# Seven more pairs of warming products in the prologue of an mLSTM and feed-forward kernel

## The chip, the cores and the metric

The kernel runs on one core of a Trainium2 chip. The metric is the device time of one execution, in microseconds (us). Before the change the median of three runs is 470.69 us.

## The reference

Four batches of eight heads run an mLSTM over 768 tokens with a head size of 40. Its gated output, 3072 tokens of 320 channels, goes through a feed-forward block with 2048 hidden channels and a leaky activation.

```python
for t in range(S):
    m_new = np.maximum(f_gate[:, :, t] + m, i_gate[:, :, t])
    f_stab = np.exp(f_gate[:, :, t] + m - m_new)
    i_stab = np.exp(i_gate[:, :, t] - m_new)
    m = m_new
    C = f_stab[:, :, None, None] * C + i_stab[:, :, None, None] * np.einsum('bhd,bhe->bhde', vt, kt)
    n = f_stab[:, :, None] * n + i_stab[:, :, None] * kt
    h_tilde = np.einsum('bhde,bhe->bhd', C, qt)
    nq = np.einsum('bhd,bhd->bh', n, qt)[:, :, None]
    denom = np.maximum(np.abs(nq), 1.0)
    y[:, :, t] = (1.0 / (1.0 + np.exp(-o_gate[:, :, t]))) * h_tilde / denom
# y becomes x: (B*S, H*D)
h = x @ w_in
out = (np.maximum(h, 0.0) + alpha * np.minimum(h, 0.0)) @ w_out
```

## The kernel before

The tokens are cut into chunks of 128, six to a batch. For a chunk the recurrence is written as products: scores (keys by queries) weighted by decays, times the values, plus what the state at the chunk's start gives. Two chunks form a group of 256 tokens, and each group then goes through the feed-forward block, whose products are each split into high and low parts (`WH`, `WL`, `OH`, `OL`, `XH`, `XL`, `gh`, `gl`).

Every engine works through its instructions in a fixed order. The string `ORDER` names the steps of the first six chunks and the first two groups in the order in which they are issued, a repeated `PATTERN` goes on from there, and `pin` chains all instructions in that order. A step may issue instructions on several engines; each engine runs its own in the order of the string, and waits on the others through semaphores.

The change lies in the prologue, the first 20 us or so, before any feed-forward product. Steps there, with their names in `ORDER`, the lines in the profile and the tiles:

- `warm2` issues two bf16 products of the identity with itself, 128 x 256, into a PSUM tile `warm` (L152) that nobody reads. `warm18` issues 18 at the very start.
- `qT0`, `kT0`, `qT1`, `kT1`: transposes of a chunk's queries or keys on TensorE (L245, tile `pqk`). `qc1`, `kc1`: their copies on ScalarE (L987, L301, L302; tiles `qf`, `kf`).
- `sp01`, `sp00`, `sp11`, `sp10`: the spreads of the decays. The digits are the chunk and the parity of the heads. Each is one bf16 "bar" product over 512 columns with full rows (L92) that blanks the future, and four float32 products that spread a row of `g_L` over the partitions, with 32 rows (L1001; the trace has two records for each); both go into a tile `pb`.
- `ex01` and the like: the exponentials of a spread on ScalarE (L1030, tile `E`).
- `bTt`, `wTt`, `eTt`: small transposes of the gates (L959, tiles `ps_gb`, `ps_gw`, `ps_ge`), and `bTc`, `wTc`, `eTc`: their copies on VectorE (L963, tile `gates`).
- `L1` (VectorE, L1111), `wd0` (the weighted keys `kd`, L160), `i00j` (unpacking a piece of `w_in`, VectorE L816), `gmd` (`g_gd`, VectorE L1139) and `gmm` (its product `pg` on TensorE, L1146).
- `sc00`, `sc01`, `sc11`, `sc10`: the scores (L1055, tile `pS`, with 104 rows). `um0`: the first state update (L182, tile `pu`), `uc0` its copy (VectorE, L196, tile `C`).

Tiles `pqk`, `pb`, `ps_g*`, `pu`, `pg` share four PSUM buffers in turn. The tile `warm` has a buffer of its own.

The warming products come from these lines:

```python
    def dense(dst, k):
        x = ident.bitcast(BF16)
        for _ in range(k):
            nc.tensor.matmul(dst[:, : 2 * P], x[:, :P], x, start=True, stop=True)
```

Of the kernel before, what the change touches and what calls it, by code (L numbers as in the profile page):

```python
# [17 lines left out]
def kernel(ctx: ExitStack, tc: tile.TileContext, q, k, v, i_gate, f_gate, o_gate, w_in, w_out, alpha, out):  # L18
# [575 lines left out]
    def first_stacks():  # L594
# [25 lines left out]
    OBA = range(0)  # L620
    FILL = {}
    ORDER = """warm18 dq0 Cz warm2 warm2 warm2 qT0 warm2 sca0 lf0a kT0 i00d lf0z lf0b li0 L0 sca1 bj0 dq1 warm2 qc0 kc0 sp01 eeL i00s
        lf1a wt0 qT1 qc1 bTt bTc ex01 sp00 sp11 r0d lf1b ewj wTt wTc ex00 sp10 ex11 kT1 i00y L1 li1 do0 dv0 kfz i01d
        eTt ex10 wd0 dq2 gma i00j sc00 o0d lpa sc01 um0 kc1 gmd gmm sc11 eTc eel bj1 og1 r0s uc0 fm1 wtl wg01 sc10 ewl
        lpb i11d wd1 alT wg00 gmc qT2 i01s glt ft1 wg10 glc alC dL lpc lpd lpe qc2 warm2 wg11 dv1 um1 uc1 i00h i01x
        i01j kT2 kc2 i00p o0s o0x sp20 v0 r0y r0j gr0 sp21 fm2 dq3 ex20 warm2 o0j r0h i01h ft2 i01p ex21 o0h warm2 gg0
        r0l gx0 i11s sc20 wg20 v1 ta1 gr1 qT3 qc3 i11x gp0 x0 xa0 sc21 dL4 gg1 gx1 gp1 kT3 wg21 x1 xa1 o1d wd3 xd0 r0H
        xd1 wd2 sq30 ey30 r0L i11j ex40 o0l F0 U00 i20d i10d R00 S00 kc3 v2 ta2 um2 uc2 o1s o1y U01 dq4 i10s i10x i10j
        sq31 gr2 o1j i11k i11l ey31 qT4 G00 ex41 fm3 ft3 sc30 K00 wg30 i10h um3 uc3 D00 R01 kT4 i20s do1 S01 qc4 wd4
        kc4 o1h i20x sc31 wg31 dv2 um4 uc4 i20j og2 o2d i20h gg2 i10p fm4 o1l o5d sc41 wg41 G01 K01 i21d gx2 r2d sc40  # L630
        i20p o2s o2x dq5 wg40 o5s o5x v3 ta3 o2j gr3 gg3 o2h o5j r2s dL5 o4d r2x o2l U02 o3d r2j gx3 gp3 R02 gp2 i21s
        v4 ft4 ta4 qT5 qc5 r2H ex50 r2h r2p U03 x2 R03 S02 G02 x3 dq6 i21y i21j r2L i31d fm5 ft5 xa2 xd2 i21h i21p dv3
        i30d kT5 kc5 K02 S03 o4s o4y D01 G03 wd6 K03 o3s o3y o3j D02 do2 dL7 ex51 o7d o4j o6d U04 R04 S04 o3h xa3 V05
        r05 o3p o4h sc50 o4p sc51 G04 i31s i31x xd3 s05 wg51 um6 uc6 K04 gr4 wg50 F1 U10 U11 R10 S10 og3 gg4 gx4 dL6
        gp4 R11 S11 G10 o5h o5p v5 K10 D10 U12 ta5 G11 g05 K11 vp0 i31j i30s i30x gr5 gg5 U13 i31h i30j R12 i30h D11
        S12 i31l G12 gx5 gp5 K12 D12 R13 dq7 S13 o7s i30l U06 o7x do3 o7j N05 G13 K13 D13 tp0 o6s tp1 o6x R06 tp2 x4
        x5 o6j o6h vp1 U07 o7h tp3 D03 D04 D05 R07 S06 G06 S07 o6l xa5 xd5 xa4 xd4 G07 K06 K07 D06 o7l D07 Z0"""
    PATTERN = """og.-1 ua.0 m1.0 V4<< tf.1 ub.0 vb.1 xn.-1 V5<< tg.1 g2<< m0.0 N2<< vc.1 c1.0 r4<< vb.0 d1.0 xp.-1 th.1 h1.0 ti.1 uc.0
        s4<< ud.0 D2<< ue.0 U6<< g4<< l1.0 g3<< N3<< uf.0 r5<< lG.-1 c0.0 vd.1 X:-1 vc.0 ua.1 lG.2 sh.1 ub.1 s5<< N4<<
        oa.0 R6<< d0.0 g5<< ug.0 h0.0 l0.0 uc.1 V7<< N5<< xa:-1 vd.0 D3<< D4<< D5<< S6<< ta.2 tb.2 xb:-1 uh.0 lL.2  # L640
# [687 lines left out]
```

## Time and profile before

| what | value |
| --- | --- |
| median of 3 runs | 470.69 us (470.62 to 471.09) |
| profiled execution: time | 472.36 us |
| profiled execution: span | 470.7 us |
| mean granted TensorE clock over the span | 0.989 |
| TensorE busy (products; weight loads) | 464.5 us; 452.1 us |
| VectorE, ScalarE, GpSimd busy | 310.1, 314.4, 308.7 us |
| bytes moved by DMA | 61.61 MB |

The span runs from the first to the last instruction of the profiled execution; its time includes what lies around the span. Engines in the profile's rows: PE is TensorE, DVE VectorE, ACT ScalarE, POOL GpSimd, SP SyncE, which issues the transfers here. A row such as `pb<-g_L,ident` names the tile written and the tiles read. "Idle before" in brackets is how long the engine had stood still and who released it. The granted clock is the share of TensorE's full clock that the throttle let through. Products are pipelined, so that the ends that the timeline models overlap a little; in the chain of waits they are cut to what each adds.

### The profile page before, as it was taken

The page shows a single profiled execution, that of the slowest core. Times are in us where ns is not written, and L with a number is a line of the kernel's source. Part 1 is how long each engine was busy: PE and PEld are TensorE (multiplying, and loading weights), DVE is VectorE, ACT ScalarE, POOL GpSimd, SP SyncE. Part 2 cuts the span into 40 slices and gives each one's busy share as a digit, 9 for nine tenths or more (in the row PEclk, how much of TensorE's full clock was granted, in tenths as well). Part 3 has the DMA queues.
Part 4 walks back from the last instruction along what each step waited for, and adds up shares of the span by engine and source line. Part 5 has one row for each costly group of instructions (what it writes and reads, how often), then busy time and mean ns, then how long its engine had stood idle before and what let it go on. Part 6 is the DMA issues. An engine that isn't in the chain of part 4 may idle for free.

```text
span 470.7 us, 11787 instructions
## 1 busy us (share of the span) xinstructions
PE 464.5 (99%) x4420; PEld 452.1 (96%) x4420; DVE 310.1 (66%) x659; ACT 314.4 (67%) x714; POOL 308.7 (66%) x398
## 2 busy tenths in 40 slices
PE   8999999999999999999999999999999999999997
PEld 6899999999999999999999999999999999999996
DVE  4589899767875775775675675676576676663321
ACT  4778998868858658559659659558658658423332
POOL 7634657664789589479689589479689586324231
PEclk9599999999999999999999999999999999999999
DMA  9996997659683574688583584579672352000000
GB/s 171 244 246 126 225 272 227 122 121 222 124 176 98 122 163 112 116 185 171 122 164 109 125 149 124 116 158 187 134 155 90 95 110 64 1 29 1 29 2 28
DMA packets 156163, 61.61 MB, mean 131 GB/s; under 512 B 140154, under 2 KB 145834, under 8 KB 156106
## 3 DMA queue, kind: packets, MB, share of 16 engines
q1 hardware_dynamic: 156026, 60.75, 58.6%
q8 instruction: 35, 0.57, 0.5%
q14 instruction: 22, 0.18, 0.1%
q10 hardware_dynamic: 80, 0.11, 0.1%
HBM read 36.90 MB, written 4.03 MB: 87 GB/s over the span
## 4 chain that ended last, share of the span: by engine, by line
PE 92%; DVE 3%; ACT 2%; DMA 1%; issue 1%; SPq 1%; DVEq 0%; ACTq 0%
PE po L733 35%; PE ph L696 6%; PE ph L701 5%; PE ph L702 5%; PE ph L699 5%; PE ph L697 5%; PE ph L698 5%; PE ph L700 5%; PE ph L703 5%; PE pH L360 4%; PE pS L461 3%; PE pS L1055 2%; PE pu L182 2%; PE pH L321 1%; PE p L550 1%; PE pI L385 1%
## 5 line engine op out<-in xcount | busy, mean ns | idle before, releaser
L722 POOL TENSOR_TENSOR gl<-g,gh 128x512 fp32r<-128x512 f32 x74 | 95.7, 1295 | 37.9 <-ACT gh L720 30.9
L733 PE MATMUL po<-OH,gh 128*128 128x320 f32 x368 | 110.7, 312 | 0.0
L733 PE MATMUL po<-OL,gh 128*128 128x320 f32 x368 | 109.3, 309 | 0.0
L706 ACT ACTIVATE g<-ph 128x512 f32<-128x512 f32 x96 | 57.3, 597 | 76.1 <-PE ph L703 71.9
L711 DVE SCALAR_TENSOR_TENSOR g<-g,oma,ph 128x256 f32<-128x256 f32 x148 | 63.6, 471 | 36.0 <-ACT g L706 36.0
L733 PEld LDWEIGHTS po<-OH,gh 128*128 128x128 f32 x368 | 69.1, 188 | 0.0
L733 PE MATMUL po<-OH,gl 128*128 128x320 f32 x368 | 69.1, 309 | 0.0
L733 PEld LDWEIGHTS po<-OL,gh 128*128 128x128 f32 x368 | 69.1, 188 | 0.0
L696 PE MATMUL ph<-XH,WH 128*128 128x256 f32 x192 | 58.0, 302 | 0.4 <-DVE g L711 0.4
L733 PEld LDWEIGHTS po<-OH,gl 128*128 128x128 f32 x368 | 57.9, 188 | 0.3 <-DVE gl L722 0.3
L701 PE MATMUL ph<-XL,WH 128*128 128x256 f32 x192 | 54.3, 283 | 0.0
L702 PE MATMUL ph<-XL,WH 128*128 128x256 f32 x192 | 54.2, 282 | 0.0
L699 PE MATMUL ph<-XH,WL 128*128 128x256 f32 x192 | 54.2, 282 | 0.0
L697 PE MATMUL ph<-XH,WH 128*128 128x256 f32 x192 | 54.1, 282 | 0.0
L698 PE MATMUL ph<-XH,WL 128*128 128x256 f32 x192 | 54.1, 282 | 0.0
L703 PE MATMUL ph<-X2L,W 128*128 128x256 f32 x192 | 53.4, 278 | 0.0
L700 PE MATMUL ph<-X,W 128*128 128x256 f32 x192 | 53.4, 278 | 0.0
L347 ACT CAST E<-pS 128x512 bf16<-128x512 f32 x72 | 41.1, 582 | 15.0 <-DVE pS L344 14.3
L432 ACT ACTIVATE E<-Lb,gates 128x128 f32<-128x128 f32 x160 | 50.1, 393 | 0.0
L720 ACT CAST gh<-g 128x512 fp32r<-128x512 f32 x74 | 44.7, 617 | 7.2 <-DVE g L711 4.8
L344 DVE TENSOR_TENSOR pS<-pS,E 128x512 f32<-128x512 f32 x36 | 25.0, 696 | 31.1 <-PE pS L461 27.5
L435 POOL TENSOR_SCALAR_AFFINE_SELECT E<-E 128x512 f32<-128x512 f32 x40 | 26.7, 667 | 20.9 <-ACT E L432 20.9
(196 smaller groups left out, 1146.0 us busy)
## 6 DMA issues: line engine op xcount, KB each, us to landing
Lb<-L_d SPq DMA_DIRECT2D x20, 512.0 KB
wo<-in_moe_w_out_dram SPq DMA_DIRECT2D x8, 640.0 KB
wi<-in_moe_w_in_dram SPq DMA_DIRECT2D x8, 512.0 KB
qn<-in_q_dram SPq DMA_DIRECT2D x24, 160.0 KB
kn<-in_k_dram SPq DMA_DIRECT2D x24, 160.0 KB
og<-in_o_gate_dram SPq DMA_DIRECT2D x24, 160.0 KB
va<-in_v_dram SPq DMA_DIRECT2D x24, 160.0 KB
out_dram<-ob SPq DMA_DIRECT2D x11, 320.0 KB
```

The lines of the kernel that those rows point to most:

```text
L696: nc.tensor.matmul(dst, WH[half][:, 0, hs], XH[:, 0], start=True, stop=False)
L697: nc.tensor.matmul(dst, WH[half][:, 1, hs], XH[:, 1], start=False, stop=False)
L698: nc.tensor.matmul(dst, WL[half][:, 0, hs], XH[:, 0], start=False, stop=False)
L699: nc.tensor.matmul(dst, WL[half][:, 1, hs], XH[:, 1], start=False, stop=False)
L700: nc.tensor.matmul(dst, W2[:, fs], X2, start=False, stop=False)
L701: nc.tensor.matmul(dst, WH[half][:, 0, hs], XL[:, 0], start=False, stop=False)
L702: nc.tensor.matmul(dst, WH[half][:, 1, hs], XL[:, 1], start=False, stop=False)
L703: nc.tensor.matmul(dst, W2[:, fs], X2L, start=False, stop=True)
L706: nc.scalar.activation(gt, ph, AF.Relu, scale=-1.0)
L711: nc.vector.scalar_tensor_tensor(out=y[:, e], in0=gt[:, e], scalar=oma[:, f : f + 1], in1=ph[:, e], op0=ALU.mult, op1=ALU.add)
L722: (nc.vector if split else nc.gpsimd).tensor_tensor(gl, y, gh.bitcast(F32), ALU.subtract)
L733: nc.tensor.matmul(po[j], x[:, e, j * P : (j + 1) * P], W[f // NB][:, f % NB], **ends)
```

## The change

Seven more `warm2` are put into `ORDER`; nothing else is changed. Three stand ahead of `qT1`, one ahead of `sp00`, two ahead of `sp11` and one ahead of `sp10`:

```diff
-        lf1a wt0 qT1 qc1 bTt bTc ex01 sp00 sp11 r0d lf1b ewj wTt wTc ex00 sp10 ex11 kT1 i00y L1 li1 do0 dv0 kfz i01d
-        eTt ex10 wd0 dq2 gma i00j sc00 o0d lpa sc01 um0 kc1 gmd gmm sc11 eTc eel bj1 og1 r0s uc0 fm1 wtl wg01 sc10 ewl
...
+        lf1a wt0 warm2 warm2 warm2 qT1 qc1 bTt bTc ex01 warm2 sp00 warm2 warm2 sp11 r0d lf1b ewj wTt wTc ex00 warm2
+        sp10 ex11 kT1 i00y L1 li1 do0 dv0 kfz i01d eTt ex10 wd0 dq2 gma i00j sc00 o0d lpa sc01 um0 kc1 gmd gmm sc11
...
```

The string takes one more line, so lines behind it count one more after the change. On VectorE, ScalarE, GpSimd and SyncE the instructions and their order stay the same; TensorE's queue gets 14 weight loads and 14 products. On TensorE, at the first of the places, from the spread of `sp01` to the spread of `sp00`, before:

```order
L1001 MATMUL pb_1_194<-g_L,ident 128x128 x4
L245 MATMUL pqk_0_205<-ident,qn_76 104x128 x4
L959 MATMUL ps_gb_212<-ident,g_WH_94 128x32 x2
L92 LDWEIGHTS ident
L92 MATMUL pb_0_221<-later,ident 128x512
L1001 MATMUL pb_0_221<-g_L,ident 128x128 x4
```

and after (a weight load and a product of `warm` stand six times ahead of the transposes and twice ahead of the bar; one of each is shown):

```order
L1002 MATMUL pb_1_194<-g_L,ident 128x128 x4
L152 LDWEIGHTS ident
L152 MATMUL warm<-ident 128x256
...
L245 MATMUL pqk_0_211<-ident,qn_76 104x128 x4
L960 MATMUL ps_gb_218<-ident,g_WH_94 128x32 x2
...
L92 LDWEIGHTS ident
L92 MATMUL pb_0_229<-later,ident 128x512
L1002 MATMUL pb_0_229<-g_L,ident 128x128 x4
```

The transposes of the second chunk's queries now stand behind three pairs, and the next bar behind a fourth. On TensorE, at the other places, from the spread of `sp00` to that of `sp10`, before:

```order
L92 MATMUL pb_1_227<-later,ident 128x512
L1001 MATMUL pb_1_227<-g_L,ident 128x128 x4
L959 MATMUL ps_gw_238<-ident,g_WL_95 128x32 x2
L92 LDWEIGHTS ident
L92 MATMUL pb_0_247<-later,ident 128x512
L1001 MATMUL pb_0_247<-g_L,ident 128x128 x4
L245 MATMUL pqk_1_258<-ident,kn_78 104x128 x4
```

and after (four weight loads and products of `warm` stand ahead of the first bar, two ahead of the second):

```order
L152 LDWEIGHTS ident
L152 MATMUL warm<-ident 128x256
...
L92 MATMUL pb_1_239<-later,ident 128x512
L1002 MATMUL pb_1_239<-g_L,ident 128x128 x4
L960 MATMUL ps_gw_250<-ident,g_WL_95 128x32 x2
...
L92 LDWEIGHTS ident
L92 MATMUL pb_0_261<-later,ident 128x512
L1002 MATMUL pb_0_261<-g_L,ident 128x128 x4
L245 MATMUL pqk_1_272<-ident,kn_78 104x128 x4
```

The bars and spreads keep their order, with two pairs and one pair put between them.

More of the change, by code (lines that the diff above doesn't have):

```diff
@@ L622 @@
     ORDER = """warm18 dq0 Cz warm2 warm2 warm2 qT0 warm2 sca0 lf0a kT0 i00d lf0z lf0b li0 L0 sca1 bj0 dq1 warm2 qc0 kc0 sp01 eeL i00s
-        lf1a wt0 qT1 qc1 bTt bTc ex01 sp00 sp11 r0d lf1b ewj wTt wTc ex00 sp10 ex11 kT1 i00y L1 li1 do0 dv0 kfz i01d
-        eTt ex10 wd0 dq2 gma i00j sc00 o0d lpa sc01 um0 kc1 gmd gmm sc11 eTc eel bj1 og1 r0s uc0 fm1 wtl wg01 sc10 ewl
-        lpb i11d wd1 alT wg00 gmc qT2 i01s glt ft1 wg10 glc alC dL lpc lpd lpe qc2 warm2 wg11 dv1 um1 uc1 i00h i01x
-        i01j kT2 kc2 i00p o0s o0x sp20 v0 r0y r0j gr0 sp21 fm2 dq3 ex20 warm2 o0j r0h i01h ft2 i01p ex21 o0h warm2 gg0
@@ L627 @@
[L627 to L636, printed above, removed]
@@ L637 @@
-        x5 o6j o6h vp1 U07 o7h tp3 D03 D04 D05 R07 S06 G06 S07 o6l xa5 xd5 xa4 xd4 G07 K06 K07 D06 o7l D07 Z0"""
+        lf1a wt0 warm2 warm2 warm2 qT1 qc1 bTt bTc ex01 warm2 sp00 warm2 warm2 sp11 r0d lf1b ewj wTt wTc ex00 warm2
+        sp10 ex11 kT1 i00y L1 li1 do0 dv0 kfz i01d eTt ex10 wd0 dq2 gma i00j sc00 o0d lpa sc01 um0 kc1 gmd gmm sc11
+        eTc eel bj1 og1 r0s uc0 fm1 wtl wg01 sc10 ewl lpb i11d wd1 alT wg00 gmc qT2 i01s glt ft1 wg10 glc alC dL lpc
+        lpd lpe qc2 warm2 wg11 dv1 um1 uc1 i00h i01x i01j kT2 kc2 i00p o0s o0x sp20 v0 r0y r0j gr0 sp21 fm2 dq3 ex20
@@ new lines @@
+        warm2 o0j r0h i01h ft2 i01p ex21 o0h warm2 gg0 r0l gx0 i11s sc20 wg20 v1 ta1 gr1 qT3 qc3 i11x gp0 x0 xa0 sc21
+        dL4 gg1 gx1 gp1 kT3 wg21 x1 xa1 o1d wd3 xd0 r0H xd1 wd2 sq30 ey30 r0L i11j ex40 o0l F0 U00 i20d i10d R00 S00
+        kc3 v2 ta2 um2 uc2 o1s o1y U01 dq4 i10s i10x i10j sq31 gr2 o1j i11k i11l ey31 qT4 G00 ex41 fm3 ft3 sc30 K00
+        wg30 i10h um3 uc3 D00 R01 kT4 i20s do1 S01 qc4 wd4 kc4 o1h i20x sc31 wg31 dv2 um4 uc4 i20j og2 o2d i20h gg2
+        i10p fm4 o1l o5d sc41 wg41 G01 K01 i21d gx2 r2d sc40 i20p o2s o2x dq5 wg40 o5s o5x v3 ta3 o2j gr3 gg3 o2h o5j
@@ new lines @@
+        r2s dL5 o4d r2x o2l U02 o3d r2j gx3 gp3 R02 gp2 i21s v4 ft4 ta4 qT5 qc5 r2H ex50 r2h r2p U03 x2 R03 S02 G02 x3
+        dq6 i21y i21j r2L i31d fm5 ft5 xa2 xd2 i21h i21p dv3 i30d kT5 kc5 K02 S03 o4s o4y D01 G03 wd6 K03 o3s o3y o3j
+        D02 do2 dL7 ex51 o7d o4j o6d U04 R04 S04 o3h xa3 V05 r05 o3p o4h sc50 o4p sc51 G04 i31s i31x xd3 s05 wg51 um6
+        uc6 K04 gr4 wg50 F1 U10 U11 R10 S10 og3 gg4 gx4 dL6 gp4 R11 S11 G10 o5h o5p v5 K10 D10 U12 ta5 G11 g05 K11 vp0
+        i31j i30s i30x gr5 gg5 U13 i31h i30j R12 i30h D11 S12 i31l G12 gx5 gp5 K12 D12 R13 dq7 S13 o7s i30l U06 o7x
@@ L638 @@
+        do3 o7j N05 G13 K13 D13 tp0 o6s tp1 o6x R06 tp2 x4 x5 o6j o6h vp1 U07 o7h tp3 D03 D04 D05 R07 S06 G06 S07 o6l
+        xa5 xd5 xa4 xd4 G07 K06 K07 D06 o7l D07 Z0"""
     PATTERN = """og.-1 ua.0 m1.0 V4<< tf.1 ub.0 vb.1 xn.-1 V5<< tg.1 g2<< m0.0 N2<< vc.1 c1.0 r4<< vb.0 d1.0 xp.-1 th.1 h1.0 ti.1 uc.0
```

## The prediction

> **What bounds the kernel now.** I read the page first, for the chain of waits and the granted clock over the span.
>
> ```profile
> PEclk9599999999999999999999999999999999999999
> ...
> PE 92%; DVE 3%; ACT 2%; DMA 1%; issue 1%; SPq 1%; DVEq 0%; ACTq 0%
> ```
>
> The chain that ends last is 92% TensorE, so a microsecond taken out of TensorE's queue is a microsecond of the kernel, unless another engine stands right behind. The clock is full in all slices of 11.77 us but the second, which reads 5 tenths. The view by stretches, for TensorE alone, says when. I cut it where the granted clock changes and went on in the same steps of 3.41 us (columns: stretch, its length, TensorE's busy time and instructions, granted clock, DMA share, GB/s):
>
> ```profile
> 8.25:11.67 3.42, 2.83 (x21) 1.00 1.12 192
> 11.67:15.08 3.41, 3.41 (x13) 0.50 1.04 150
> 15.08:18.49 3.41, 3.41 (x15) 0.50 1.09 258
> 18.49:21.91 3.42, 3.42 (x22) 0.50 0.98 295
> ...
> 25.32:28.73 3.41, 3.41 (x44) 1.00 1.13 210
> ```
>
> The clock is halved for three steps, 11.67 to 21.91 us, while TensorE is busy all the time. So it is not idleness as the profile counts it that took the clock away. What TensorE did in those steps stands in the chain of waits (start, length, what):
>
> ```profile
> 9.38 0.62 PE pqk L245 x4
> 9.99 0.24 PE ps_gb L959 x2
> 10.24 0.32 PE pb L92
> 10.56 1.08 PE pb L1001 x8
> 11.64 0.49 PE pb L92
> 12.13 2.00 PE pb L1001 x8
> 14.14 0.16 PE ps_gw L959 x2
> 14.30 0.54 PE pb L92
> 14.84 2.00 PE pb L1001 x8
> 16.84 1.02 PE pqk L245 x4
> 17.86 0.24 PE ps_ge L959
> 18.10 3.71 PE pS L1055 x16
> 21.82 0.49 PE pu L182 x15
> 22.30 0.50 PE pg L1146 x2
> ```
>
> From 9.38 us TensorE is the chain without a gap. The same instruction shows the clock: eight records of L1001 take 1.08 us before the fall and 2.00 us in it. The step before the fall holds transposes (pqk, ps_gb), spreads over 32 of the array's 128 rows (L1001), and one bar product with full rows (L92). After it the clock comes back only when the step from 18.49 us is almost all score products (pS), with 104 rows. My reading: the clock follows how much of the array works, and spreads and transposes count little. That is inferred from these rows; the profile names no cause.
>
> Prices at full clock come from the same chain some microseconds later:
>
> ```profile
> 24.75 0.93 PE pS L1055 x8
> ...
> 25.84 0.57 PE pqk L245 x4
> ...
> 26.75 0.22 PE warm L152 x2
> ...
> 28.04 0.22 PE pb L92
> ```
>
> **The change part by part.** TensorE alone gets instructions: seven pairs, 14 products with 14 weight loads. The queues of VectorE, ScalarE, GpSimd and SyncE and what they wait for are as before; no DMA is added or moved. A pair costs 0.22 us at full clock (the warm row) and about 0.44 us at half, by the ratio of the L1001 rows; the latter is an estimate.
>
> *The first three pairs* stand ahead of the second chunk's query transposes, which waited for their data:
>
> ```profile
> 9.38 0.62 PE L245 MATMUL pqk<-ident,qn 128*104 128x128 f32 x4 [0.58 <-DMA qn<-in_q_dram]
> ```
>
> Three pairs are 0.66 us; the gap is 0.58 and the pipelined end of the spread before it takes some of that, so they cost between 0 and 0.1 us. I take 0.05. Were the data there earlier, they would cost the full 0.66.
>
> *The other four pairs* (one ahead of each of the two bars at 10.24 and 14.30, two ahead of the bar at 11.64) meet no gap in the chain. They cost 4 x 0.22 = 0.88 us if the clock holds.
>
> *What the clock gives.* The trace of before does not show whether the pairs hold the clock. The nearest rows: the step 8.25 to 11.67, at whose end the clock fell, has 0.22 us of full-row work (its L92, priced by the later row) beside spreads and transposes; the step 25.32 to 28.73, which kept 1.00, has a warming pair, a bar, and otherwise transposes and short small products, thus 0.44 us of dense work and some more. With the change the first step has four pairs and a bar, 1.10 us, and the next one three pairs and two bars, again 1.10. Both are above the step that held. One row speaks against: 11.67 to 15.08 has two bars (0.49 and 0.54 us at half clock) and did not bring the clock back, so winning it back needs more than keeping it. The end at "no effect" is worth nothing and costs the pairs; the end at "held throughout" is worth what follows. I take "held", since the new steps lie on the side of the step that held.
>
> At full clock the chain from 11.64 us on shrinks: the bar 0.49 to about 0.25 (0.24 saved), the spread 2.00 to 1.08 (0.92), the next bar 0.54 to 0.25 (0.29), the next spread 0.92 again, the transposes 1.02 to 0.57 (0.45), sixteen score records 3.71 to 2 x 0.93 (1.85). Sum 4.67. Less 0.93 for the pairs, TensorE alone would reach pg 3.74 us earlier, at 18.56 instead of 22.30.
>
> *What is late next.* pg multiplies a tile that VectorE makes, and VectorE's queue does not shrink with TensorE's clock (start, length, operation, idle time before and its releaser):
>
> ```profile
> 14.34 0.23 DVE L963 COPY gates<-ps_gw 128x64 f32<-128x64 f32 x1 [3.84 <-PE ps_gw L959]
> ...
> 16.32 1.74 DVE L816 SCALAR_TENSOR_TENSOR t_wi<-wi,t_wi 128x512 uint32<-128x512 uint32 x1
> 18.12 1.70 DVE L1139 TENSOR_TENSOR g_gd<-ident,g_gam 32x192 f32<-32x192 f32 x1
> 19.74 0.17 DVE L963 COPY gates<-ps_ge 128x32 f32<-128x32 f32 x1
> 22.36 0.67 DVE L196 COPY C<-pu 40x168 f32<-40x168 f32 x2 [2.45 <-PE pu L182]
> ```
>
> VectorE works without a pause (the rows left out show no idle time) from the weights' copy (14.34) to g_gd's end at 19.82. That copy waits for ps_gw, before which the change saves 0.24 + 0.92 and adds 0.05 + 3 x 0.22 = 0.71: it comes 0.45 us earlier. So g_gd ends at 19.82 - 0.45 = 19.37, pg starts at about 19.4 instead of 22.30, and TensorE stands about 0.85 us in front of it. VectorE's idle 2.45 us ahead of the copy of C shrinks to about nothing, since that copy may follow at 19.5. The gain at pg is 2.9 us, the smaller of 3.74 and 2.9.
>
> *Whether it carries to the end.* ScalarE stands idle for the next transposes from TensorE, and the DMA queue stands behind a tile whose maker (GpSimd's weighted keys) is itself downstream of TensorE:
>
> ```profile
> 26.51 0.59 ACT L987 COPY qf<-pqk 104x512 f32<-104x512 f32 x1 [3.15 <-PE pqk L245]
> SPq L98 <- POOL kd L160: 10.3, 1, 10.3
> ```
>
> ScalarE's last work ahead of 26.51 ended at 23.36; it too moves up, since its decays follow the spreads, so a shift of 2.9 us leaves it waiting still. The 10.3 us wait of SyncE says that the later loads are held back by compute and would start earlier with it. I count the gain as kept in full.
>
> Sum: 2.9 us off. The profiled execution took 472.36 us for a span of 470.7; it should become 469.5 and 467.8. The median of the three runs, 470.69, lies 1.67 us below that execution's time; from it, 470.69 - 2.9 = 467.8 us.
>
> [...]
>
> **The rivals.**
>
> *The pairs don't hold the clock (slower).* If what decides is not the share of dense work, or needs more of it than 1.10 us in a step, the fall comes at 11.67 us as before and the pairs are queue time: 0.05 + 0.22 ahead of it, three pairs at 0.44 in it, 1.6 us in all, 472.3 us. If the scores are pushed so far that a fourth step runs at half, it is up to 1.7 us more. It decides if the spread at sp11, the second after the change's first gap, still takes 2.00 us. For it: the steps at half clock that had two bars and stayed low. Against it: the step from 25.32.
>
> *The clock holds in part.* One step of 3.41 us at half clock costs TensorE up to 1.7 us; ahead of pg up to 0.85 of that falls into its new wait. The gain is then 1.2 to 2.0 us, 468.7 to 469.5, and with two such steps 470.5. For it: the new steps are above the one that held by my count of dense work, but the count of the small products in that one is rough. [...]
>
> *The gain is used up behind pg.* If ScalarE or a load is late in place of TensorE between 26 and 74 us, between 0 and 2.9 us are kept; near 470.7 at the worst. Against it stand the two rows above.
>
> *More than forecast.* VectorE's two long rows, 1.74 and 1.70 us, may shorten if GpSimd's work falls elsewhere beside them. TensorE's own limit is 3.74 us, 466.95.
>
> **How the numbers follow.** Held, with 2.9 us (2.4 to 3.74): 0.62. In part: 0.17. Used up behind: 0.07. Not held: 0.14. The time is that of the first, 467.8. The range runs from TensorE's own limit, 466.9, to 471.0, which takes in the partial cases and the used-up one and leaves out the slower rival and a rest; the likeliest case alone would span 466.9 to 468.3. What a measurement here can tell from no change is about 0.2%, 0.94 us. Faster by more: 0.62 and 0.13 of the partial case, 0.75. Within: 0.04 and 0.07 and a rest of the slower rival, 0.12. Slower: 0.13.
>
> **What would show it.** Right: a granted clock of 1.00 in every step; L1001's groups of eight at 1.08 us each; the score group near 1.9; TensorE idle some 0.85 us ahead of pg, with VectorE's g_gd as releaser; the next transposes' copy on ScalarE near 23.6; all later rows shifted by one amount. Wrong in the mechanism: a clock of 0.50 in any of the three steps. Wrong downstream: the clock holds, pg comes near 19.4, and the shift has shrunk by 74 us.

## The result, and the profile after

The changed kernel took 469.32 us (median of 19 executions, 468.63 to 470.74), the kernel before, run beside it, 471.04 us (median of 19, 470.57 to 476.63). The ratio is 0.994 with a 95% interval of 0.9917 to 0.9963: 2.8 us faster, between 1.7 and 3.9; the means lie 2.8 us apart, the medians 1.72. The profiled execution took 468.76 us for a span of 467.0. Ratios here and below leave out the executions that lie over 1.5% above the fastest of their kernel; there are none in this comparison, and the first experiment shows what those of the kernel before are.

The page of the changed kernel, its span, the clock in forty slices and the shares of the chain of waits:

```profile
span 467.0 us, 11815 instructions
...
PEclk9999999999999999999999999999999999999999
...
PE 93%; DVE 4%; ACT 2%; issue 1%; POOL 0%; POOLq 0%; DVEq 0%; ACTq 0%
```

The half-speed slice is gone. The same stretches as before the change, TensorE alone:

```profile
8.25:11.67 3.42, 3.42 (x28) 1.00 1.10 188
11.67:15.08 3.41, 3.41 (x27) 1.00 1.14 155
15.08:18.49 3.41, 3.34 (x39) 1.00 1.10 250
18.49:21.91 3.42, 3.24 (x26) 1.00 0.76 212
```

In the last three of these steps TensorE was busy throughout before the change, at half clock; now it has its full clock there, and even stands idle for a little. In the first, the gap of 0.58 us is filled. The chain of waits of the changed kernel through the place of the change:

```profile
8.63 0.76 PE warm L152 x6
9.39 0.44 PE pqk L245 x4
9.83 0.24 PE ps_gb L960 x2
10.07 0.32 PE warm L152 x2
10.40 0.22 PE pb L92
10.62 1.08 PE pb L1002 x8
11.70 0.54 PE warm L152 x4
12.24 0.21 PE pb L92
12.46 1.08 PE pb L1002 x8
13.81 0.15 DVE t_wi L809
13.96 0.18 issue
14.14 1.21 DVE g_L L1112
15.35 0.38 DVE kd L160
15.73 1.68 DVE t_wi L817
17.41 1.12 DVE g_gd L1140
18.67 0.54 PE pg L1147 x2
```

The three pairs end at 9.39 us, where the transposes started before too (9.38), so they lie in the gap. Each group of eight spread records takes 1.08 us. Behind the second of them the chain leaves TensorE for VectorE, from the unpacking to `g_gd`, and comes back at pg, at 18.67 us instead of 22.30. TensorE's own row for pg and ScalarE's copy of the next transposes, from the timeline:

```profile
18.67 0.54 PE L1147 MATMUL pg<-g_gd,unit 32*104 32x192 f32 x2 [0.25 <-DVE gates L964]
22.92 0.59 ACT L988 COPY qf<-pqk 104x512 f32<-104x512 f32 x1 [1.13 <-PE pqk L245]
```

ScalarE now waits 1.13 us there instead of 3.15 and starts 3.59 us earlier. Further on, the last piece of VectorE's work in the chain ahead of a long run of TensorE's, before and after, from the chains of waits of the two kernels:

```profile
73.58 0.49 DVE g L711
```

```profile
69.97 0.48 DVE g L712
```

The shift is 3.63 us at pg, 3.59 at that copy and 3.61 here: it is kept in full.

### The profile page after: what moved, and what is told of

It reads as the page before. It is cut to its first block, busy times and chain, and to the rows that moved or that the text cites. A ratio compares the mean times of both kernels' runs of the same rounds, so it can differ in the third digit from the quotient of the medians.

```text
span 467.0 us, 11815 instructions
## 1 busy us (share of the span) xinstructions
PE 461.4 (99%) x4434; PEld 449.5 (96%) x4434; DVE 308.0 (66%) x659; ACT 314.6 (67%) x714; POOL 309.4 (66%) x398
## 4 chain that ended last, share of the span: by engine, by line
PE 93%; DVE 4%; ACT 2%; issue 1%; POOL 0%; POOLq 0%; DVEq 0%; ACTq 0%
PE po L734 36%; PE ph L697 6%; PE ph L702 5%; PE ph L703 5%; PE ph L700 5%; PE ph L698 5%; PE ph L699 5%; PE ph L704 5%; PE ph L701 5%; PE pH L360 4%; PE pS L461 4%; PE pu L182 2%; PE warm L152 2%; PE pH L321 1%; PE p L550 1%; PE pI L385 1%
```

## The experiments

Theory A, my reading of the two traces: the granted clock changes in steps of 3.41 us (before the change it was full from 4.84 to 11.67 us and halved from there to 21.91, which is two and three of them), what counts in a step is how much of the array works, and the edges of the steps fall differently in every execution; the pairs lift most possible steps above what holds the clock. Rivals: TensorE must only not stand idle (C), or the executions differ by something else than the clock (B).

**The kernel before, again.** No edit.

> The kernel before, run again for the granted clock of each of its executions. The question is why the median fell by only 1.7 us while the two profiled executions lie 3.6 us apart. Theory A (the phase of the throttle's steps): executions differ in how many steps of 3.41 us run at half clock; each step takes 0.0036 off the mean clock (3.41 / 2 / 470), so times fall into groups: about 470.7 us at a mean of 0.993 (two steps), about 472.3 at 0.989 (three steps), about 475 at 0.982 to 0.985 (four or five). Theory B (the clock is the same in all, 0.989, and the groups come from the transfers): the mean clock is 0.989 in all executions whatever their time.

Ninety executions of the kernel before, from this and the later comparisons, and forty of the changed kernel, by their mean granted clock:

| kernel | mean clock | executions | times, us |
| --- | --- | --- | --- |
| before | 0.991 to 0.993 | 31 | 470.6 to 471.1 |
| before | 0.988, 0.989 | 17 | 471.5 to 472.4 |
| before | 0.982 | 21 | 474.8 to 475.3 |
| before | 0.978 | 16 | 476.1 to 476.9 |
| before | 0.964 | 5 | 482.4 to 482.9 |
| after | 0.999, 1.000 | 37 | 468.6 to 469.9 |
| after | 0.996 | 3 | 470.7 to 470.8 |

The ratio of this kernel to itself is 1.0002 (0.9961 to 1.0044). Time follows the clock in groups, as theory A says, though it did not foresee the last two groups; B is out. The profiled execution of this run took 474.93 us; its stretches, cut at its own edges:

```profile
5.79:9.20 3.41, 3.41 (x29) 1.00 1.28 222
9.20:12.62 3.42, 3.42 (x26) 1.00 1.18 193
12.62:16.03 3.41, 3.41 (x14) 0.50 1.18 208
...
26.27:29.68 3.41, 3.41 (x23) 0.50 1.07 215
29.68:33.10 3.42, 3.42 (x46) 1.00 0.99 354
```

The clock falls at 12.62 us instead of 11.67 and stays down for five steps, to 29.68. In the two steps ahead of that fall TensorE was never idle (3.41 of 3.41 and 3.42 of 3.42 us): here the second chunk's transposes start at 8.94 us, right behind the spread, without the gap of 0.58 us. So the gap is not in every execution, and here the clock fell without it. No execution of the ninety kept its clock (the highest mean is 0.993). Their median is 472.2 and their mean 473.7 us; the forty of the changed kernel have 469.3 for both.

**Only the three pairs in the gap.**

```diff
-        lf1a wt0 qT1 qc1 bTt bTc ex01 sp00 sp11 ...
+        lf1a wt0 warm2 warm2 warm2 qT1 qc1 bTt bTc ex01 sp00 sp11 ...
```

> Only the three pairs in the 0.58 us gap ahead of the second chunk's transposes; the four between the spreads are left out. Theory A (share of the array's rows at work): the step that ended at 11.67 us now has 0.66 + 0.22 us of dense work and may hold, but the next one has only its two bars, so the clock is halved one step later and for about two steps instead of three; 0 to 1.5 us under the kernel before, mean clock 0.992 to 0.995. Theory C (TensorE must not stand idle): the gap was the cause, it is closed, and the clock holds throughout: 0.999, as fast as the full change or 0.9 us faster, since four pairs are saved.

Median 469.20 us (12 executions, 468.55 to 483.65), ratio 0.9934 (0.9887 to 0.9981). Seven executions have a clock of 0.996 or more and 468.55 to 469.20 us; five have 0.993 down to 0.964 and 471.8 to 483.65. In the profiled one (473.72 us) TensorE was busy throughout both steps ahead of the fall, 8.11 to 14.94 us (3.42 of 3.42 and 3.41 of 3.41), and the clock fell all the same, so C is out as the whole cause; the gain foreseen under A, a fall one step later in general, was too low for seven and too high for the others. Its chain of waits, with the edge at 14.94 us:

```profile
13.33 1.08 PE pb L1001 x8
14.41 0.58 PE pqk L245 x4
14.99 0.24 PE ps_ge L959
15.23 3.71 PE pS L1055 x16
```

The fall came three steps after the clock was raised (4.70 us), just ahead of the scores, which then ran at half clock: 3.71 us for sixteen records.

**The seven pairs on 32 rows.** The pairs multiply 32 rows instead of 128, at the same places.

```diff
+        def thin(n=1):
+            x = ident.bitcast(BF16)[:BH]
+            for _ in range(n):
+                nc.tensor.matmul(junk[:, : 2 * P], x[:, :P], x, start=True, stop=True)
```

> The full change, but each of the seven pairs works on 32 of the 128 rows: the same number of products and columns and the same time on TensorE, a quarter of the array. Theory A: the clock falls as in the kernel before, mean 0.989 to 0.993, and the pairs are pure queue time: 1 to 1.6 us slower than the kernel before. Theory C (busy time of TensorE is what counts, with whatever rows): the clock holds at 0.999 and the time is that of the full change, some 1.7 to 2.8 us under the kernel before.

Median 474.42 us, ratio 1.006 (1.0018 to 1.0102): slower than the kernel before, and by more than the 1 to 1.6 us expected: 2.3 in the median. No clock of the twelve executions is above 0.989, and eight are below; the fastest takes 473.38. The chain of waits (L1082 is the thin pairs) and the step of the fall:

```profile
12.24 0.44 PE warm L1082 x4
12.68 0.33 PE pb L92
13.01 1.92 PE pb L1002 x8
...
19.32 3.71 PE pS L1056 x16
```

```profile
13.05:16.46 3.41, 3.41 (x15) 0.50 0.99 208
```

Two pairs take 0.44 us at full clock, as two `warm` pairs do (31.61 in the kernel before), TensorE was busy for all of the 3.41 and 3.42 us of the two steps ahead, and the clock falls at 13.05 us. Between these two kernels the rows that the pairs fill made the difference, not TensorE's busy time: with 128 rows 37 of forty executions had a clock of 0.999 or more, with 32 rows none of twelve. This is the kernel that my slower rival described, at 473.4 us and more against the 472.3 worked out there.

**The seven pairs as transposes.** Each pair is two float32 transposes of the identity.

```diff
+        def turn(n=1):
+            for _ in range(n):
+                nc.tensor.transpose(junk[:, :P], ident, ident)
```

> The full change, but each pair is two float32 transposes of the identity, full 128 rows and 128 columns, about 0.11 to 0.14 us each at full clock, 0.25 for two. It tells whether transposes count as work for the clock. Theory A with transposes not counted: the clock falls as before, mean 0.989 to 0.993, time 1 to 2 us above the kernel before. Theory A with transposes counted like other full-row products: it holds, mean 0.999, time within 0.5 us of the full change. [...]

Median 469.29 us (468.70 to 471.10), ratio 0.993 (0.9896 to 0.9964). Nine of twelve executions have 0.999 or more, three 0.996, none less. The profiled execution's chain (L1081 is the transposes) and its two steps there:

```profile
8.39 0.80 PE warm L1081 x6
...
11.53 0.59 PE warm L1081 x4
```

```profile
8.06:11.48 3.42, 3.42 (x27) 1.00 1.15 193
11.48:14.89 3.41, 3.41 (x26) 1.00 1.25 167
```

Full-row transposes of the identity held the clock in these two steps (1.00 in both) and at 0.999 or more in nine of the twelve executions.

**The full change again, and without the gap's pairs.** The first is the changed kernel; the second leaves out the three ahead of `qT1`.

> The full change again, beside the three kernels below, for the granted clock of each execution. Theory A (steps of 3.41 us whose edges fall differently in every execution; the pairs lift the dense work of nearly every possible step above what holds the clock): mean clock 0.999 to 1.0 and 468.6 to 469.6 us in nine of ten executions, now and then one step at half clock (0.996, near 470.7). Rival: the first result was luck of the edges, and here too a third of the executions have two or more steps at half clock, with times above 471 us.

> The four pairs between the spreads alone, without the three in the gap ahead of the second chunk's transposes. Theory A: the work ahead of 9.4 us is again thin (a bar, a spread over 32 rows, a gap of 0.58 us), so the clock falls at the same edges as before the change where an edge lies between 10 and 12 us, and holds in the executions whose edges lie otherwise; times between the full change and the kernel before, with a mean clock of 0.989 to 0.996 in at least half of them. Rival (the four between the spreads do all of it, the three in the gap are free but of no use): 0.999 in nine of ten, and the times of the full change.

The full change: median 469.38 us, ratio 0.9906 (0.9868 to 0.9944); eight of nine executions at 0.999 or more, one at 0.996. The profiled one is the latter:

```profile
13.37:16.78 3.41, 3.41 (x27) 1.00 1.20 249
16.78:20.19 3.41, 3.41 (x16) 0.50 0.80 150
```

An edge at 16.78 us closes a step with one pair and one bar, the spreads and the transposes, and the next one runs at half clock. Seven pairs don't cover every edge.

Without the gap's pairs: median 469.25 us (8 executions). Five executions held (468.56 to 469.27), three had 0.978 and 477.5 to 477.9 us. The mean of all eight is 472.2 us, against 469.5 for the nine of the full change; the ratio, 0.989 (0.9834 to 0.9947), is that of the five. Chain of waits of one of the three, with the edge at 11.74 us:

```profile
10.61 1.08 PE pb L1002 x8
11.70 0.89 PE warm L152 x4
12.59 0.43 PE pb L92
13.01 2.00 PE pb L1002 x8
```

The four pairs then cost double, 0.89 us for two of them against 0.44 at full clock, and save nothing: the spread behind them takes 2.00 us. Neither part alone is safe: five of twelve executions fell to 0.993 or less with the gap's pairs alone, three of eight without them. I had expected half or more of them to fall, to 0.989 to 0.996; three of eight fell, and further.

**Five pairs.** Without the one ahead of `sp00` and one of the two ahead of `sp11`.

> Five of the seven pairs: without the one ahead of the bar of chunk 0 and one of the two ahead of the first bar of chunk 1. Theory A with each pair as 0.22 us of queue ahead of the small transposes on which VectorE's next work waits: where the clock holds, 0.3 to 0.45 us faster than the full change (468.2 us at best); where the dense work no longer suffices, one or more steps at half clock in a quarter to a half of the executions. Rival (five are as safe as seven): the clock at 0.999 in nine of ten and a median 0.3 to 0.4 us under the full change.

Median 469.15 us (6 executions); five held (468.73 to 469.26), one had 0.982 and 476.67, and the ratio, 0.989 (0.9841 to 0.994), is that of the five. They average 469.00 us, the eight of the full change that held beside them 469.35: the 0.3 to 0.45 us that I expected from the shorter queue may be there, but the times of either kernel spread by more than that, and the fastest of the full change in all its runs (468.63) is no slower. On the risk, six executions decide nothing.

**The unpacking later.** VectorE's 1.75 us piece ahead of `g_gd` moves behind the copy of pg.

```diff
-        ... gma i00j sc00 o0d ... alT wg00 gmc qT2 ...
+        ... gma sc00 o0d ... alT wg00 gmc i00j qT2 ...
```

> The full change, and the unpacking of a piece of w_in on VectorE (1.75 us, ahead of g_gd) moved behind the copy of pg. It tests whether VectorE's queue is what pg waits for after the change. Theory: VectorE's chain to g_gd gets 1.1 us shorter, TensorE's wait ahead of pg goes, and pg starts 0.3 us earlier; all later rows shift by it, 0.3 us faster than the full change in executions of the same clock. Rival: VectorE's state weighting or the ScalarE copy of the unpacked piece gets late instead, 0 to 1 us slower than the full change.

> The full change with the unpacking moved later, again, beside the other two of this call, to count its groups: 468.2 to 468.5 us with an early first edge, 0.7 us more with a late one, and one execution in ten with a step at half clock. Rival: the first result had early edges by luck, and the median is that of the full change, 469.3.

> The full change, a third time, as the measure for the two others of this call: 468.6 to 468.8 us with an early first edge, 469.2 to 469.6 with a late one, 470.7 with a step at half clock; 0.3 to 0.4 us above the kernel with the unpacking moved later, group by group.

Median 468.40 us (6 executions, ratio 0.9881, 0.9835 to 0.9926), where the full change beside it had 469.38, and 468.50 the second time (12 executions, ratio 0.9928, 0.99 to 0.9956), where the full change had 469.15 (12 executions, ratio 0.9918, 0.9884 to 0.9951). VectorE's rows in the first:

```profile
16.34 0.54 DVE L1140 TENSOR_TENSOR g_gd<-ident,g_gam 32x192 f32<-32x192 f32 x1 [0.81 <-ACT g_gam L1137]
...
20.46 0.68 DVE L817 SCALAR_TENSOR_TENSOR t_wi<-wi,t_wi 128x512 uint32<-128x512 uint32 x1
```

`g_gd` is done by 16.9 instead of 18.5 us, with its row at 0.54 us instead of 1.19, and pg starts without a wait behind TensorE's own work, at 18.23. So VectorE's queue was what bounded the gain at pg, which starts 0.44 us earlier than in the first profile of the change alone: 0.19 of it VectorE's chain had gained already at its start (13.48 instead of 13.67), by an earlier end of the opening, and the other 0.25 is TensorE's wait that is gone (0.3 expected). The unpacking takes 0.68 us there instead of 1.75. The fastest executions take 468.23 and 468.20 us, against 468.98 and 468.70 with the change alone beside them, and the medians are 0.98 and 0.65 us lower: this version is faster than the kernel before and than the change alone. How much of the difference of the medians is the edges of the steps is open.

**A shorter opening.** As the last, with `warm14` instead of `warm18`.

> The full change with the unpacking moved later, and four fewer warming products at the very start (14 instead of 18). The profiles so far show the clock raised between 4.5 and 6.9 us, as the edges fall; where it is raised late, the 24 products at the start end at 6.7 instead of 5.7 us and the rows behind them come up to 0.9 us later. Theory: four products of 0.21 us less at half clock take back up to 0.85 us in executions with a late edge and nothing in those with an early one, whose next transposes wait for their data anyway; the two groups of times, 0.7 us apart, close up near 468.3 us. Rival: the opening work no longer raises the clock at the late edges, and some executions run a whole step more at half clock, 1 us or more slower.

Median 468.42 us (12 executions, 468.07 to 469.88; ratio 0.992, 0.989 to 0.9949) against 468.50 for the kernel without this edit beside it: not told apart. The reason for the edit is in the chains of the full change in its second run, raised at 6.54 us, and of the kernel with the unpacking later, raised at 4.52:

```profile
1.43 5.27 PE warm L152 x24
```

```profile
1.43 4.28 PE warm L152 x24
```

Where the clock comes late the opening takes 1 us more; that accounts for at least a part of the spread of 1.3 us among executions that never fell. One execution in twelve and two in twelve, without and with the edit, had a step at half clock.

## Why the prediction was right or wrong

*Direction and mechanism: right.* The clock holds, the spreads take 1.08 us, the sixteen score records 2.05 in the timeline, and the chain passes to VectorE ahead of pg, as the sum had it. (The row of pg names as releaser the small copy L964 right behind `g_gd`, where I had named `g_gd`; both are VectorE's.)

*The starting point: wrong, and it is the main error.* The sum was made on an execution with three steps at half clock (mean 0.989, 472.36 us), and its gain was taken off the median of three executions which, by the groups above, had a clock near 0.993. The prediction gave the difference of 1.67 us and did not ask what it was: it was part of the gain already. From the execution it belongs to, 472.36 less the measured shift of 3.6 us is 468.76, the changed kernel's profiled time to the digit. From the median it gave 467.8 where 469.32 was measured. That the range still held 469.32 is owed to the width put in for the partial and used-up cases; the likeliest case alone, 466.9 to 468.3, missed it. The median even lies among the times of the partial rival, 468.7 to 469.5, although 17 of the 19 executions held.

*The size at pg: 2.9 forecast, 3.63 measured.* VectorE's `g_gd` took 1.19 us instead of the 1.70 of its row before, and its chain started at 13.67 us, where 13.89 was forecast, as the transposes behind the three pairs take 0.44 us in the chain instead of 0.62. TensorE's wait was 0.25 us, not 0.85. That VectorE's long rows might shorten if GpSimd's work fell elsewhere stood among the rivals, not in the sum, and GpSimd's rows fit that, before and after:

```profile
17.60 1.37 POOL L951 TENSOR_TENSOR g_WL<-g_WH,g_L 32x512 f32<-32x512 f32 x1
18.94 0.66 POOL L1158 TENSOR_TENSOR L_rest<-g_L,LP 32x256 f32<-32x256 f32 x1
```

```profile
16.94 1.37 POOL L952 TENSOR_TENSOR g_WL<-g_WH,g_L 32x512 f32<-32x512 f32 x1
17.33 1.19 DVE L1140 TENSOR_TENSOR g_gd<-ident,g_gam 32x192 f32<-32x192 f32 x1
```

`g_gd` ends 0.2 us behind an operation of GpSimd each time: behind the second before (19.82 after 19.60), behind the first after (18.52 after 18.31). It doesn't take the change: the kernel before, run again, has 1.21 us for the row too, behind one operation. This error of 0.73 us and the one of the starting point, 1.67, work against each other: 467.8 + 1.67 - 0.73 is 468.74.

*The pairs' price: right for this execution.* The three in the gap cost next to nothing (9.39 against 9.38 us); in one without the gap, as in the first experiment, they would be queue time, as the prediction said; their row in the chain is 0.76 us. The next three take 0.32 and 0.54 us in the chain, but the bars behind them 0.22 and 0.21 instead of the 0.32 of a bar without a pair ahead (10.24 in the kernel before): some 0.65 net, 0.22 each.

*The carry: right.* 3.63, 3.59 and 3.61 us at three places.

*The reading of the throttle: half right.* That 32-row products such as the spreads count little is borne out here by the thin pairs, with which no execution of twelve was above 0.989. That transposes count little is refuted here for transposes of the identity, with which nine of twelve had 0.999 or more; whether those of data count alike was not tried. So my 1.10 us of dense work in a step was no measure that could be relied on.

*The partial rival* is real: three of forty executions had one step at half clock and came out at 470.7, some 1.5 us above the mean of the others; from 472.36 that is a gain of 1.65, within the 1.2 to 2.0 us that it gave, but its times, taken from the median, were too low. The clock was raised at 4.84 us (the kernel before), 5.79 (the same again), 6.54 (the full change again) and 6.90 (five pairs), though the first product starts at 1.43 us in the first and in the last two alike. I gave this rival 0.17, with three times at hand that lay within 0.47 us; ninety show a spread of 12 us.

## What to carry to other kernels

Where the granted clock halves while TensorE is busy, as here from 11.67 to 21.91 us, look at how many rows its products fill, and try full-row products: here seven pairs of them kept it at 0.999 or more in 37 of forty executions, the same pairs on 32 rows in none of twelve. Try them first in gaps that a transfer leaves: three pairs in the gap of 0.58 us put the transposes back by 0.01 us here (9.38 to 9.39). The gap's pairs alone held it in only part of the executions here, so that the others had to be paid for in the chain. Such a change is one of chances: list the mean clock of many executions, and subtract a gain only from an execution of the same clock as the one on which it was worked out. Look for the next bound among the engines that did not get slower with TensorE's clock, here VectorE: its unpacking took 1.74 us while that clock was halved and 1.75 while it was full, its `g_L` 1.20 and 1.21, and TensorE then waited 0.25 us for it at pg.

## What the runs showed of the hardware

The times here were measured in the prologue of this kernel and its variants, each in one profiled execution. The clock stayed halved for 3.41 us in the full change's second run (16.78 to 20.19), 10.24 in the kernel before (11.67 to 21.91) and with the thin pairs (13.05 to 23.29), 13.65 with the gap's pairs alone (14.94 to 28.59), 17.06 in the kernel before run again (12.62 to 29.68) and 20.48 without the gap's pairs (11.74 to 32.22): one, three, four, five and six times 3.41.

In the run with the gap's pairs alone the scores (104 rows) filled 3.12 of the 3.41 us from 14.94 to 18.35, and the clock was not raised until 28.59; in the kernel before they filled 3.33 of 3.42, from 18.49, and it was raised at 21.91. In the run with thin pairs scores filled hardly more than in the first, 3.16 of the 3.42 us from 19.87, but the rest was state updates (128 rows) instead of transposes, and the clock was raised at 23.29. In the run with five pairs the opening's products start at 1.43 us and the clock was raised at 6.90; up to 3.49, a step of 3.41 us earlier, they had filled 2.06 us, and it was not raised there. In the run with the unpacking later they start at 1.43 too, and it was raised at 4.52, after 3.09 us of them. And the pairs held the clock, at 0.999 or more in 37 of forty executions, although both operands are the identity, almost all zeros.

VectorE's unpacking took 1.74 us in the kernel before and 1.75 in the changed one, where it lay beside a GpSimd operation (16.16 to 17.52 us, and 15.49 to 16.86). A piece of the same shape took 0.69 us in both where GpSimd stood idle (29.89 us, and 26.29), and the moved one 0.68 (20.46, in the run with the unpacking later).
